# A decode kernel's first weight load, split by partitions over two DMA queues

## The chip, the cores and the metric

The kernel runs on one core of one Trainium2 chip. The metric is device time in microseconds (us), from one launch. The kernel before was run three times: 126.8, 126.88 and 127.03 us, median 126.88 us. A further execution was taken with the hardware profiler; its own time is 126.89 us, and all durations below are from it.

## The reference

One token `x` of 576 numbers is normalised (`xn`), sent through two branches, and their sum with `x` is the output. Everything is bfloat16.

```python
# attention branch: 32 query heads, 16 key/value heads, the last W = 4096 of 65536 cached rows
q = (xn @ wq)                        # wq: 576 x 4096
k, v = k_cache[:, :, Sk - W:, :], v_cache[:, :, Sk - W:, :]   # 16 heads x 4096 x 128 each
p = softmax(q . k * Dh ** -0.5);  o = p . v
attn = o @ wo                        # wo: 4096 x 576
# gated MLP branch
z = gelu(xn @ w_in)                  # w_in: 576 x 4608
z1, z2 = z[:2304], layernorm(z[2304:])
mlp = (z1 * (w_sp * z2 + b_sp)) @ w_out   # w_out: 2304 x 576
out = x + attn + mlp
```

There is one token, so every weight and every cached key and value is read once and used for one vector. The kernel reads 50.96 MB from memory.

## The kernel before

**What is loaded.** All the large loads are issued on one queue, SP's (`nc.sync.dma_start`, in the helpers `rows`, line 82, and `load_kv`, line 88). Each covers all 128 partitions with one contiguous row per partition. In order: the first 2 of each partition's 9 half rows of `wq` (8 KB per partition, 1 MB in all, tile `rest`), the other 7 half rows (28 KB per partition, tile `wq`), the key groups `k0` and `k1` (32 KB per partition, 4 MB each), `w_in` in two loads (tiles `win` and `rest`), `k2`, `v0`, `k3`, `v1`, `v2`, `v3`, `w_out` and, in five loads, `wo`. These 18 loads share four slots of SBUF (tags a, b, c, d), so that a later load waits on SP until the last reader of its slot is done; `k2`, for example, waits for the transposes of `k0`.

**What else is loaded.** On ACT's queue (`nc.scalar.dma_start`, lines 112 to 117) come `x`, in three pieces of 192 numbers, and the two scalars `w_sp` and `b_sp`. At the end the output leaves by the same queue (line 482).

**How the work goes.** The order on each engine is the order of the program (`tc.manual_schedule()`); nothing is moved by a scheduler. DVE clears constants and PSUM tiles (lines 123 to 170), copies `x` into `xtw` (line 181), nine small matmuls turn it into a column (line 183), and a chain of small operations (lines 187 to 209) makes the normalised `XT`. Then `wq` is multiplied, first the two half rows in `rest`, then the seven in `wq` (line 217), the query is spread (lines 222 to 245, ending in `Qb`), and per group of four heads `g` the keys are transposed on DVE in two halves (`keys`, line 258), scored (`scores`, line 265), put through the softmax (`sm_a`, `sm_b`), multiplied with the values (`pv`, line 329) and normalised (`tail`). `z_mms` (line 365) does `w_in` between groups; `out_mms` (line 465) does `w_out` and `wo` at the end and finishes as the last rows of `wo` land.

**Semaphores.** Each DMA raises one of eight semaphores, which are handed round; a DMA that gets one already used waits on its issuing engine until the earlier use has landed. In the kernel before, `k1` waits in this way for a piece of `x`.

Of the kernel before, what the change touches and what calls it, by code (L numbers as in the profile page):

```python
# [14 lines left out]
D = 576  # L15
# [11 lines left out]
NR = 98  # L27
NF = FH // 128
CUT = (0, 264, D)
XP = D // 3  # L30
EPS = 1e-5
SCALE = DH ** -0.5
GELU_C = 0.7978845608028654
# [4 lines left out]
def kernel(  # L38
# [14 lines left out]
    nc = tc.nc  # L53
    P = nc.NUM_PARTITIONS
# [16 lines left out]
    x_flat = A_x.flatten_outer_dims()  # L71


    def rows(slot, src, name, lo, n, at=None):

        w = src.shape[1]
        if at is None:
            t = big.tile([P, n * w], BF16, name=f"{name}{lo}", tag=slot)[:]
        else:
            t = slot[:, at:at + n * w]  # L80
        v = t.rearrange("p (s c) -> p s c", c=w)
        nc.sync.dma_start(v, src.rearrange("(p s) c -> p s c", p=P)[:, lo:lo + n, :])  # L82
        return [(lo + s, v[:, s, :]) for s in range(n)]

    def load_kv(slot, src, g, name):

        t = big.tile([P, TP * DH], BF16, name=f"{name}{g}", tag=slot)
        nc.sync.dma_start(t[:], src[0, GK * g:GK * g + GK, SK - W:SK, :].rearrange("h (r t) d -> r h (t d)", t=TP))
        return t[:].rearrange("p (t d) -> p t d", d=DH)

    wq_h = A_wq.rearrange("r (e c) -> (r e) c", e=2)
    win_h = B_w_in.rearrange("r (e c) -> (r e) c", e=2)
    K, V = {}, {}
    rest = big.tile([P, TP * DH], BF16, name="rest", tag="d")
    wq_sb = rows(rest, wq_h, "wq", 0, 2, 0) + rows("a", wq_h, "wq", 2, 7)
    K[0] = load_kv("b", A_k_cache, 0, "k")
    K[1] = load_kv("c", A_k_cache, 1, "k")
    win_sb = rows("a", win_h, "win", 0, 7) + rows(rest, win_h, "win", 7, 2, 4096)
    K[2] = load_kv("b", A_k_cache, 2, "k")
    V[0] = load_kv("c", A_v_cache, 0, "v")  # L100
# [3 lines left out]
    V[3] = load_kv("c", A_v_cache, 3, "v")  # L104
    ends = [big.tile([P, TP * DH], BF16, name=f"end{n}", tag="ad"[n]) for n in range(2)]
    wout_sb = rows(ends[0], B_w_out, "wout", 0, NF, 0)
    wo_sb = []
    for n, t, at in ((14, 1, 0), (9, 1, 14), (6, 0, NF), (2, 0, NF + 6), (1, 0, NF + 8)):
# [1 line left out]


    xrow = const.tile([1, D], BF16, name="xrow")
    for n in range(3):
        nc.scalar.dma_start(xrow[:, XP * n:XP * (n + 1)], x_flat[:, XP * n:XP * (n + 1)])
    spb = const.tile([1, 2], BF16, name="spb")
    nc.scalar.dma_start(spb[:, 0:1], B_w_sp.flatten_outer_dims()[0:1, 0:1])
# [396 lines left out]
```

## Time and profile before

| what | value |
|---|---|
| median of three runs | 126.88 us (126.8 to 127.03) |
| the profiled execution's own time | 126.89 us |
| its span, first to last instruction | 125.1 us |
| read from memory | 50.96 MB, 407 GB/s over the span |
| busy: PE, DVE, ACT, POOL | 70.8, 78.5, 43.2, 7.1 us |
| first load: issued, landed | 0.73 us, 4.8 us after issue |
| second load (`wq`): issued, landed | 1.15 us, 12.8 us after issue |
| `x` in use on DVE from | 7.32 us |
| `XT` ready, first `wq` matmul | 12.57 us |

Times inside the profile count from the span's start. The span is 1.8 us shorter than the execution's own time; what lies around it is launch and end. A DMA has three stages in the profile: the issuing engine works on the instruction (SPq or ACTq), the 16 DMA engines move packets (here one packet per partition row, and one of 4 bytes per DMA and engine that raises the semaphore), and the waiting engine goes on after the landing. The profile names the DMA queues by number: q1 is SP's, q10 is ACT's, q8 and q14 are instruction fetches. "DMA share" is the time that packets took as a share of 16 engines; a packet's bytes are counted where it starts, so in short windows the figures jump.

### The profile page before, as it was taken

How to read it: one execution, taken by the hardware profiler on the slowest of the kernel's cores; microseconds unless marked ns; L12 is line 12 of the kernel's file. 1: busy time of each engine (PE TensorE's matmuls, PEld its weight loads, DVE VectorE, ACT ScalarE, POOL GpSimd, SP SyncE). 2: the span in 40 equal slices, each digit the busy share in tenths (PEclk: the TensorE clock that was granted, in tenths of full speed). 3: DMA queues.
4: the chain of work that ended last, by engine and by line, in shares of the span. 5: the costliest groups of instructions: out<-in, count | busy, mean ns of one | idle time of the engine just before them, and what ended most of it. 6: DMA issues, size and time to landing. Idle time of an engine off the chain costs nothing.

```text
span 125.1 us, 1617 instructions
## 1 busy us (share of the span) xinstructions
PE 70.8 (57%) x626; PEld 28.9 (23%) x626; DVE 78.5 (63%) x150; ACT 43.2 (34%) x101; POOL 7.1 (6%) x19
## 2 busy tenths in 40 slices
PE   0012841009878469998390992059892932049992
PEld 0001201001101013998000131002211411015850
DVE  6745025899799976308999367999938359003301
ACT  2100011000000956996069008707801941940001
POOL 2961000000000000000000000000000100000000
PEclk9999998555995867755559599657998555555899
DMA  4999899998999999898999989999999999999960
GB/s 118 511 422 440 385 471 440 398 492 356 487 420 402 385 493 461 377 492 372 461 451 398 482 367 477 401 451 430 409 482 398 451 394 440 418 413 416 428 237 0
DMA packets 2611, 51.06 MB, mean 408 GB/s; under 512 B 299, under 2 KB 428, under 8 KB 684
## 3 DMA queue, kind: packets, MB, share of 16 engines
q1 hardware_dynamic: 2592, 50.96, 95.2%
q8 instruction: 5, 0.08, 0.2%
q14 instruction: 2, 0.02, 0.0%
q10 hardware_dynamic: 12, 0.00, 0.0%
HBM read 50.96 MB, written 0.00 MB: 407 GB/s over the span
## 4 chain that ended last, share of the span: by engine, by line
DMA 61%; DVE 30%; PE 5%; SPq 1%; issue 1%; ACT 0%; DVEq 0%
DMA k<-in_A_k_cache_dram 37%; DMA end<-in_A_wo_dram 25%; DVE kT L258 22%; DVE pt L303 4%; PE S L265 3%; PE acc L465 1%; SPq L82 1%; DVE mx L286 1%; DVE on L343 1%; DVE om L339 1%; PE yps L350 0%; ACT res L481 0%; DVE rs L320 0%; DVE mt L275 0%; DVE mb L281 0%
## 5 line engine op out<-in xcount | busy, mean ns | idle before, releaser
L265 PE MATMUL S<-kT,Qb 128*8 128x512 bf16 x128 | 32.5, 1148 | 23.3 <-DVE kT L258 22.8
L258 DVE STREAM_TRANSPOSE kT<-k 128x1024 f32<-128x1024 f32 x32 | 36.8, 1207 | 6.5 <-DMA k<-in_A_k_cache_dram 6.5
L292 ACT ACTIVATE pz<-S,nm 32x1024 bf16<-32x1024 f32 x16 | 19.1, 1192 | 33.6 <-DVE nm L289 20.6
L306 ACT COPY PT<-pt 32x128 f32<-32x128 f32 x64 | 19.8, 309 | 17.2 <-DVE pt L303 16.5
L329 PE MATMUL ops<-v,PT 128*32 128x512 bf16 x128 | 11.0, 505 | 6.8 <-ACT PT L306 6.8
L265 PEld LDWEIGHTS <-Qb 128*8 128x8 bf16 x128 | 3.5, 96 | 45.0 <-issue 34.8
L303 DVE STREAM_TRANSPOSE pt<-pz 128x1024 f32<-128x1024 f32 x8 | 9.4, 1210 | 0.8 <-ACT pz L292 0.8
L339 DVE SCALAR_TENSOR_TENSOR om<-ops,rs,dmask 128x512 f32<-128x512 f32 x4 | 3.0, 750 | 10.5 <-PE ops L329 10.3
L365 PEld LDWEIGHTS <-win 128*128 128x128 bf16 x126 | 7.9, 165 | 1.9 <-issue 1.9
L365 PE MATMUL zps<-XT,win 128*128 128x2 bf16 x126 | 8.0, 202 | 0.0
L286 DVE TENSOR_REDUCE mx<-S 128x1 f32<-128x1024 f32 x4 | 4.9, 1214 | 3.9 <-PE S L265 3.9
L329 PEld LDWEIGHTS <-PT 128*32 128x32 bf16 x128 | 3.7, 117 | 11.5 <-ACT PT L306 6.9
L226 ACT CAST q_rep<-qps 128x512 bf16<-128x512 f32 x2 | 1.2, 586 | 14.9 <-DVE q_rep L228 14.9
L404 POOL TENSOR_TENSOR mz<-mz,mhalf 128x1 f32<-128x1 f32 x1 | 0.6, 554 | 85.5 <-DVE mz L403 85.5
L183 PE MATMUL ps_x<-ones_b,xtw 1*128 1x1 bf16 x9 | 0.4, 162 | 8.7 <-DVE xtw L181 8.7
L465 PE MATMUL acc<-end,Y 128*1 128x312 bf16 (+1 forms) x64 | 4.9, 285 | 0.3 <-DMA end<-in_A_wo_dram 0.3
L228 DVE CAST q_rep<-qps 128x512 bf16<-128x512 f32 x2 | 1.4, 692 | 5.1 <-PE qps L217 4.5
L481 ACT CAST res<-acc 1x312 bf16<-1x312 f32 x1 | 0.4, 411 | 11.7 <-PE acc L465 11.7
L350 PE MATMUL yps<-on,sel 128*32 128x32 f32 x32 | 2.0, 210 | 4.1 <-DVE on L343 4.1
L343 DVE TENSOR_REDUCE on<-om 128x128 f32<-128x512 f32 x4 | 4.2, 1042 | 0.1
L480 DVE CAST res<-acc 1x264 bf16<-1x264 f32 x1 | 0.4, 420 | 5.2 <-PE acc L465 5.2
L465 PE MATMUL acc<-end,hv 128*1 128x264 bf16 (+1 forms) x36 | 3.6, 360 | 0.0
(92 smaller groups left out, 56.6 us busy)
## 6 DMA issues: line engine op xcount, KB each, us to landing
k<-in_A_k_cache_dram SPq DMA_DIRECT2D x4, 4096.0 KB
v<-in_A_v_cache_dram SPq DMA_DIRECT2D x4, 4096.0 KB, 26.0
win<-in_B_w_in_dram SPq DMA_DIRECT2D x1, 4032.0 KB, 27.1
wq<-in_A_wq_dram SPq DMA_DIRECT2D x1, 3584.0 KB, 12.8
end<-in_B_w_out_dram SPq DMA_DIRECT2D x1, 2592.0 KB, 22.3
end<-in_A_wo_dram SPq DMA_DIRECT2D x1, 2016.0 KB
end<-in_A_wo_dram SPq DMA_DIRECT2D x1, 1296.0 KB
rest<-in_B_w_in_dram SPq DMA_DIRECT2D x1, 1152.0 KB
```

Of the source, the lines that this page charges most:

```text
L258: nc.vector.transpose(dst[:, 1024 * n:1024 * (n + 1)], src[:, 1024 * n:1024 * (n + 1)])
L265: nc.tensor.matmul(S[g % 2][32 * x:32 * x + 8, c, :], lhsT=Qb[:, GK * g + x, be].rearrange("p a h -> p (a h)"), rhs=kv[:, be // 2, be % 2, x],
L286: nc.vector.tensor_reduce(out=mx[:, 0:1], in_=s[:], op=ALU.max, axis=mybir.AxisListType.XY)
L292: nc.scalar.activation(pz[lo:hi, :, :, x, :], s[lo:hi].rearrange("p a (t r e) -> p (a t) r e", r=8, e=2), ACT.Exp, bias=nm[lo:hi, 0:1], sc ...
L303: nc.vector.transpose(dst[:, 1024 * n:1024 * (n + 1)], src[:, 1024 * n:1024 * (n + 1)])
L306: nc.scalar.copy(PT4[32 * a:32 * a + 32, :, x, :], pt[32 * x:32 * x + 32, :, 2 * a:2 * a + 2])
L329: nc.tensor.matmul(ops[32 * q:32 * q + 32, :], lhsT=d["PT"][:, t0 // 2:t0 // 2 + 2].rearrange("p t x h e -> p (t x h e)"), rhs=V[g][:, t0: ...
L339: nc.vector.scalar_tensor_tensor(out=om[:].rearrange("p c d -> p (c d)"), in0=ops[:], scalar=d["rs"][:, 0:1], in1=dmask[:].rearrange("p c ...
L343: nc.vector.reduce_sum(on[:], om[:].rearrange("p c d -> p d c"), axis=AXX)
L350: nc.tensor.matmul(yps[32 * g:32 * g + 32, :], lhsT=sel[:, dq, :], rhs=d["on"][:, 32 * dq:32 * dq + 32], start=(dq == 0), stop=(dq == 3), ...
L365: nc.tensor.matmul(zps[:, :, t], lhsT=wt[:, t, :], rhs=XT[:, s, :], start=(s == 0 and t == 0), stop=(s == NS - 1 and t == NF - 1), skip_gr ...
L465: nc.tensor.matmul(acc[n], lhsT=lhs[:, col:col + 1], rhs=wv[:, CUT[n]:CUT[n + 1]], start=False, stop=last, tile_position=(0, 32 * n))
```

## The change

The first load is issued as two: partitions 80 to 127 (48 rows) on ACT's queue and partitions 0 to 79 (80 rows) on SP's. ACT's part stands ahead of `x` on ACT's queue. `x` comes in two pieces of 288 numbers where it came in three of 192, so the number of DMAs is the same as before. Nothing is computed differently. The lines behind the helper move by two.

```diff
-XP = D // 3
+XP = D // 2
...
-    def rows(slot, src, name, lo, n, at=None):
+    def rows(slot, src, name, lo, n, at=None, queues=((nc.sync, 0, P),)):
...
-        nc.sync.dma_start(v, src.rearrange("(p s) c -> p s c", p=P)[:, lo:lo + n, :])
+        sv = src.rearrange("(p s) c -> p s c", p=P)
+        for q, p0, p1 in queues:
+            q.dma_start(v[p0:p1], sv[p0:p1, lo:lo + n, :])
...
-    wq_sb = rows(rest, wq_h, "wq", 0, 2, 0) + rows("a", wq_h, "wq", 2, 7)
+    wq_sb = rows(rest, wq_h, "wq", 0, 2, 0, ((nc.scalar, 80, P), (nc.sync, 0, 80))) + rows("a", wq_h, "wq", 2, 7)
...
-    for n in range(3):
+    for n in range(2):
         nc.scalar.dma_start(xrow[:, XP * n:XP * (n + 1)], x_flat[:, XP * n:XP * (n + 1)])
```

In the order of the changed program, every other instruction of every engine stands where it stood. On SP, the issue of `k1` waits for one of the two first loads, whose semaphore it takes over, where it waited for a piece of `x`; `v1` waits in addition for the landing of one of the two scalars.

## The prediction

> **What bounds the kernel now.** I read the page's slices first, then its queues, then the chain that ended last in order of time, then the start in the timeline.
>
> From the page, the span in 40 slices, and its list of queues (packets, MB, share of 16 engines):
>
> ```profile
> DMA  4999899998999999898999989999999999999960
> GB/s 118 511 422 440 385 471 440 398 492 356 487 420 402 385 493 461 377 492 372 461 451 398 482 367 477 401 451 430 409 482 398 451 394 440 418 413 416 428 237 0
> ...
> q1 hardware_dynamic: 2592, 50.96, 95.2%
> ```
>
> The DMA engines are busy from the second slice to the last but one; only the first slice (3.1 us) is half empty. Nearly everything they do is SP's queue, q1.
>
> From the chain in order of time (start, length, what), its seven longest pieces:
>
> ```profile
> 1.62 22.00 DMA k<-in_A_k_cache_dram
> 23.65 9.14 DVE kT L258 x8
> 32.81 23.86 DMA k<-in_A_k_cache_dram
> 56.69 4.62 DVE kT L258 x4
> 64.32 4.55 DVE kT L258 x4
> 78.18 4.53 DVE kT L258 x4
> 90.41 30.86 DMA end<-in_A_wo_dram
> ```
>
> The long DMA pieces do not wait for an issue; they wait in line. `k2`, issued at 32.81, lands at 56.67, 23.86 us later, though its 4.19 MB take 10 us at the 407 GB/s of the page. The rest of the time is what was queued ahead of it. So the end is the start of the stream, plus 50.96 MB at its pace, plus the tail behind the last landing (121.27 to 125.1). A delay of the stream at its start moves everything by its own size: the landing of `k2`, for which DVE has waited 5.4 us (the longest of DVE's three waits for keys), so the DVE chain behind it, and the last rows of `wo`. Compute ahead of `k2` has slack instead, 5.4 us there.
>
> The change touches the first 5 us. The timeline has:
>
> ```profile
> 0.73 1.04 ACTq L114 DMA_DIRECT2D xrow<-in_A_x_dram  x3
> 0.73 0.37 SPq L82 DMA_DIRECT2D rest<-in_A_wq_dram  x1
> 1.15 0.42 SPq L82 DMA_DIRECT2D wq<-in_A_wq_dram  x1
> ...
> 7.32 1.34 DVE L181 COPY xtw<-xrow 1x1152 bf16<-1x1152 bf16 x1 [1.31 <-DMA xrow<-in_A_x_dram]
> ...
> 12.57 1.02 PE L217 MATMUL qps<-rest,XT 128*2 128x512 bf16 x8 [0.83 <-DVE XT L208]
> ```
>
> and the start cut into half microseconds (the last two columns are the DMA share and GB/s):
>
> ```profile
> 1.70:2.20 0.50, 0.00 (x0) 0.00 (x0) 0.44 (x2) 0.00 (x0) 0.00 (x0) 1.00 1.33 246
> 2.20:2.70 0.50, 0.00 (x0) 0.00 (x0) 0.50 (x4) 0.24 (x1) 0.00 (x0) 1.00 0.61 180
> 2.70:3.20 0.50, 0.00 (x0) 0.00 (x0) 0.50 (x5) 0.50 (x1) 0.16 (x1) 1.00 0.89 360
> 3.20:3.70 0.50, 0.00 (x0) 0.00 (x0) 0.29 (x2) 0.50 (x1) 0.50 (x2) 1.00 0.97 410
> 3.70:4.20 0.50, 0.00 (x0) 0.00 (x0) 0.50 (x1) 0.04 (x1) 0.44 (x4) 1.00 1.00 426
> ```
>
> The first large packet starts at 1.73, a full microsecond after SP took up the instruction, and the stream is at its pace only from about 3. Up to 4.5 the queue list counts 0.94 MB; from 3 to 4.5 the pace was 426 GB/s, at which 0.94 MB take 2.21 us, and 2.77 us passed. **The ramp loses 0.56 us.** In the packet records the engines' first packets start spread over 1.73 to 2.15, and many of them take 0.5 to 1.05 us where an 8 KB packet takes 0.31 later. So part of the loss is the handing-out of rows to 16 engines (the spread), part is waiting for the first bytes (the length).
>
> **The change, part by part.** The sum is made against the profiled execution, 126.89 us; the median is 126.88, so nothing is to be converted.
>
> *Issue.* SP's instruction for 128 rows takes 0.37 us, those of 192 numbers on ACT 0.21 to 0.50. For 80 rows I take 0.31 (0.16 us more than the smallest for 127 more rows, scaled to 80), so 0.06 us earlier. Ends: 0 and 0.16. I take **0.06**.
>
> *Hand-out.* Two queues hand out 5 and 3 rows per engine side by side, so that each engine has work after the shorter of them. If the spread of 0.42 us goes with the number of rows, it becomes 0.42 x 48/128 = 0.16, and the mean engine starts (0.42 - 0.16)/2 = 0.13 us sooner. Ends: 0 (one shared unit hands out, or the first bytes are the limit) and 0.56 (the whole ramp goes). I take **0.13**, since the spread is the only row that is surely hand-out.
>
> *Two queues at one engine.* This is new: in the first load each DMA engine has 5 rows on q1 and 3 on q10, and will take them in turn. No row of before has two bulk queues at once, so I bound it. From below: the small packets of `x` and of the scalars on q10 (384 bytes and less) slip in between `wq` packets on q1 at no cost; a 28 KB packet of q1 ahead of or behind one takes 1.06 us like all others. So 0. From above: instruction fetches, which come on q8 and q14 between q1's packets. The 16 KB packet at 36.47 took 0.94 us (0.61 at q1's pace), and the q1 packet behind it 1.69 where its fellows took 1.19; the engine fell back by 1.41 us, 0.80 more than the bytes. The 8 KB packet on q14 at 37.31 took its 0.31, but the q1 packet behind it 1.73 for 1.19: 0.53 lost for one excursion to another queue and back. Three rows on q10 are three excursions, so the upper end is 3 x 0.80 = 2.4 us. The nearest row by size is the 8 KB one: 3 x 0.53 = 1.59. One of the three falls into the ramp, where the engines wait for first bytes anyway, which leaves **1.06 us**. All 16 engines pay it, so the stream is late by it, and no backlog makes up for it.
>
> *`x`.* ACT now issues its 48 rows first, so `x` is issued from about 1.1 instead of 0.73. In the records the first piece of before got in ahead of the bulk (1.63); the second was served only at 4.72, when engine 0 had done its first load, and the third with one `wq` packet of 1.06 us between its steps, which is why DVE waits until 7.32. Two pieces behind the first load are four packets (data and semaphore each), as many as the second and third piece of before had, at the same place in the line: again about 7.3. This hides behind nothing it needs: the `wq` multiplication has 0.38 us until `wq` lands (13.95), and if `x` comes later than that the delay runs into DVE's waits for keys, 6.5 us in all. I take 0. The two scalars follow in the same order.
>
> *Waits on SP.* `k1` waits for a first load (the one of before landed 4.8 us after its issue, at 5.5) where it waited for a piece of `x`. Behind it on SP stands `win`, which waits until 17.18 anyway, and `k1` is needed in the line only when `k0` has gone through, at 23.6. `v1` waits for a scalar that landed by 11.6, and is issued after 59. Cost 0; if SP stood until 23, the stream would run dry.
>
> *Nothing else moves*: PE gets a second landing to wait for at the first `wq` matmul, long past by 12.57.
>
> **Sum: 126.89 - 0.06 - 0.13 + 1.06 = 127.76, forecast 127.8 us.** Its own range is 127.3 (half an excursion more than the ramp hides) to 128.3 (all three paid).
>
> **The rivals.**
>
> *The ramp shrinks and the turns are free* (faster). For it: q10's small packets cost q1 nothing, and the loss at the start is real. Against it: the first packets are slow in themselves, and a second queue does not bring the first bytes sooner. If excursions cost nothing and the whole ramp scales with the rows of the shorter part, 0.56 x 48/128 = 0.21 stays and 0.35 is won, with the issue 0.41: **126.5 us** (126.2 to 126.6). It decides if every engine's share of the first load is done by about 4.5 us.
>
> *Only the issue is won* (no change). Both parts go through the same 16 engines, so the start is as before but for 0.06: **126.83 us**. [...] The `x` packets agree as far as they show that q10 runs on an engine of q1; no run here shows more.
>
> *The parts collide at their targets* (slower still). In before every load spans all partitions and the 16 engines keep 0.31 us per 8 KB row without disturbing each other. A load of fewer partitions might not. If a half of the partitions takes rows only at half the pace (213 GB/s), the 48 rows, all in the upper half, take 1.85 us, the 64 of the 80 that lie in the lower half 2.46, one behind the other 4.31 where 128 rows take 2.46 now. That is 1.85 more: 126.89 - 0.19 + 1.85 = **128.55 us**. If the two interleave well it shrinks to nothing, so it decides by how the engines pair them; nothing in the trace speaks for or against it. [...]
>
> *`x` gets stuck.* If each of its four packets waits for several `wq` packets, `x` comes up to 8 x 1.06 = 8.5 us later; DVE's waits for keys swallow 6.5 us, and 2.0 come through with the above: 129.8 us. The third piece of before passed the queue with one packet between, which speaks against it.
>
> **How the numbers follow.** Chances: turns between queues (127.8) 0.38; collision 0.14; `x` stuck 0.02; ramp shrinks 0.33; only the issue 0.13. About 0.2% (0.25 us) is what a measurement of this kernel can tell from no change, so faster is below 126.63 and slower above 127.13. Faster 0.33, same 0.13, slower 0.54. The range reaches down to take in most of the faster case and up to the collision: 126.3 to 128.6 us.
>
> **What the profile of the changed kernel would show.** The windows from 1.7 to 4.5 and the packets up to 4.5: 0.94 MB or more by then means that the ramp shrank, less that turns or collisions cost. The first load's rows on q1 and q10: lengths of 0.31 with gaps or longer packets at each change of queue bear out the forecast; lengths of 0.6 all through, the collision. The landing of `wq` (13.95 now) and of `k2` (56.67) must move by the same amount as the end; if they do not, the sum is wrong in its frame. The `xtw` copy should start near 7.3. The forecast is wrong if `wq` lands at or before 13.95, and the whole argument if the end moves without it.

## The result, and the profile after

The changed kernel takes 128.36 us (median of 5 runs, 128.16 to 128.42); the kernel before, run beside it, 127.01 us (126.8 to 127.14). The ratio is 1.0105, with a 95% interval of 1.009 to 1.012: slower by 1.35 us. The profiled execution took 128.22 us, its span is 126.4 us (before 126.89 and 125.1). Two executions among the runs below, of 139.46 and 147.88 us, were in a slower state; medians and ratios are of the others.

The start in the timeline of the changed kernel:

```profile
0.73 0.42 ACTq L84 DMA_DIRECT2D rest<-in_A_wq_dram  x1
...
0.73 0.38 SPq L84 DMA_DIRECT2D rest<-in_A_wq_dram  x1
...
1.19 0.79 ACTq L116 DMA_DIRECT2D xrow<-in_A_x_dram  x2
...
9.08 1.34 DVE L183 COPY xtw<-xrow 1x1152 bf16<-1x1152 bf16 x1 [3.08 <-DMA xrow<-in_A_x_dram]
```

SP needs 0.38 us for 80 rows where it needed 0.37 for 128: nothing is won at the issue. `x` is taken up at 9.08, 1.76 us later than before. The same start in half microseconds (DMA share and GB/s last):

```profile
1.70:2.20 0.50, 0.00 (x0) 0.00 (x0) 0.44 (x2) 0.00 (x0) 0.00 (x0) 1.00 1.66 246
2.20:2.70 0.50, 0.00 (x0) 0.00 (x0) 0.50 (x4) 0.00 (x0) 0.00 (x0) 1.00 0.39 98
2.70:3.20 0.50, 0.00 (x0) 0.00 (x0) 0.50 (x5) 0.30 (x1) 0.16 (x1) 1.00 0.89 328
3.20:3.70 0.50, 0.00 (x0) 0.00 (x0) 0.29 (x2) 0.50 (x1) 0.50 (x2) 1.00 1.07 360
3.70:4.20 0.50, 0.00 (x0) 0.00 (x0) 0.50 (x1) 0.49 (x1) 0.44 (x4) 1.00 1.13 262
4.20:4.70 0.50, 0.00 (x0) 0.00 (x0) 0.34 (x2) 0.00 (x0) 0.50 (x4) 1.00 0.89 246
4.70:5.20 0.50, 0.00 (x0) 0.00 (x0) 0.50 (x1) 0.00 (x0) 0.50 (x2) 1.00 1.08 262
5.20:5.70 0.50, 0.00 (x0) 0.00 (x0) 0.45 (x2) 0.00 (x0) 0.50 (x1) 1.00 1.00 246
```

Two things are to be seen. Up to 3.2 the start is no faster than it was: the three windows add up to 336 KB, before to 393. From 3.7 to 5.7 the stream stands at 246 to 262 GB/s, where before ran at 410 to 467 from 3.2 to 4.7, and the DMA share is still 0.89 to 1.13: the engines are not idle between packets; each packet is slow. In the packet records the 8 KB packets of that stretch last 0.46 to 0.62 us, for 0.31 before, all 16 engines at once. The last first-load packet ends at 6.36 (before 5.17), and the first packet of the second load on each engine still takes 1.41 us in the mean, for 1.06. The second load starts on the mean engine at 6.04 instead of 4.90 (1.14 later), plus 0.35 for its slow first packet: 1.49. The landing of `wq` agrees, 15.48 (issue 1.18 plus 14.3) for 13.95.

The DMA pieces among the seven longest of the chain, and DVE's waits for keys:

```profile
1.64 23.51 DMA k<-in_A_k_cache_dram
...
34.33 23.80 DMA k<-in_A_k_cache_dram
...
92.60 29.95 DMA end<-in_A_wo_dram
```

```profile
DVE kT L260 <- DMA k<-in_A_k_cache_dram: 6.8, 3, 5.4
```

`k0` lands 1.53 us later than before, `k2` 1.46, and the last packet of the stream ends 1.35 us later by the packet records. So what is lost in the first 7 us goes through to the end, as the frame of the prediction had it; and DVE still waits for keys as long as before (6.8 us, before 6.5), so that the late `x` is hidden there.

### The profile page after: what moved, and what is told of

Read it like the earlier page. It is cut to its first block, busy times and chain, and to the rows that moved or that the text cites. A ratio compares the mean times of both kernels' runs of the same rounds, so it can differ in the third digit from the quotient of the medians.

```text
span 126.4 us, 1619 instructions
## 1 busy us (share of the span) xinstructions
PE 70.4 (56%) x626; PEld 29.4 (23%) x626; DVE 78.6 (62%) x150; ACT 43.2 (34%) x101; POOL 7.0 (6%) x19
## 4 chain that ended last, share of the span: by engine, by line
DMA 61%; DVE 22%; PE 12%; SPq 2%; issue 1%; ACT 0%
DMA k<-in_A_k_cache_dram 37%; DMA end<-in_A_wo_dram 24%; DVE kT L260 18%; PE S L267 7%; PE ops L331 3%; DVE pt L305 2%; SPq L84 2%; PE acc L467 1%; PE lps L314 1%; DVE on L345 1%; DVE om L341 1%; PE yps L352 0%; ACT res L483 0%; PE acc L441 0%; DVE u L376 0%
## 5 line engine op out<-in xcount | busy, mean ns | idle before, releaser
L267 PE MATMUL S<-kT,Qb 128*8 128x512 bf16 x128 | 32.9, 1159 | 23.1 <-DVE kT L260 23.0
L331 PE MATMUL ops<-v,PT 128*32 128x512 bf16 x128 | 10.4, 479 | 6.8 <-ACT PT L308 6.8
L467 PE MATMUL acc<-end,Y 128*1 128x264 bf16 (+1 forms) x64 | 4.9, 286 | 0.9 <-DMA end<-in_A_wo_dram 0.9
L467 PEld LDWEIGHTS <-Y 128*1 128x1 bf16 x64 | 3.4, 83 | 2.3 <-issue 1.8
## 6 DMA issues: line engine op xcount, KB each, us to landing
wq<-in_A_wq_dram SPq DMA_DIRECT2D x1, 3584.0 KB, 14.3
```

The source lines that it names most:

```text
L267: nc.tensor.matmul(S[g % 2][32 * x:32 * x + 8, c, :], lhsT=Qb[:, GK * g + x, be].rearrange("p a h -> p (a h)"), rhs=kv[:, be // 2, be % 2, x],
L331: nc.tensor.matmul(ops[32 * q:32 * q + 32, :], lhsT=d["PT"][:, t0 // 2:t0 // 2 + 2].rearrange("p t x h e -> p (t x h e)"), rhs=V[g][:, t0: ...
L467: nc.tensor.matmul(acc[n], lhsT=lhs[:, col:col + 1], rhs=wv[:, CUT[n]:CUT[n + 1]], start=False, stop=last, tile_position=(0, 32 * n))
```

## The experiments

The question is why the packets are slow. The forecast said: because each engine takes turns between two bulk queues. The rival: because a load over a part of the partitions collides at its targets. Some of the expectations weigh two forms of the collision, both of them assumptions that no row of before shows. By span: each half of the partitions takes rows at half the pace. By pairing: engines that work on a partial load meet at the same small group of partitions, wherever it lies. The times of before in this section are those beside which each kernel ran, 126.84, 126.95 and 126.81 us.

**Both parts on one queue.**

```diff
-    wq_sb = rows(rest, wq_h, "wq", 0, 2, 0, ((nc.scalar, 80, P), (nc.sync, 0, 80))) + ...
+    wq_sb = rows(rest, wq_h, "wq", 0, 2, 0, ((nc.sync, 0, 80), (nc.sync, 80, P))) + ...
```

> The changed kernel with both parts of the first load (80 rows, then 48) on SP's queue; x stays in two pieces on ACT's queue. No second bulk queue is left, the two partial loads are. Turns between queues: the loss goes, about 127.0 us, and the packets of the first load last 0.31 us once the start is over. Collision of partial loads at their targets: the loss stays, packets of 0.45 us and more, 128.2 to 128.9 us.

Measured: 129.29 us, ratio 1.0182 (1.0162 to 1.0203). The second queue is gone and the loss has grown, to 2.3 us by the ratio. Its stretches, GB/s last:

```profile
3.20:4.20 1.00, 0.00 (x0) 0.00 (x0) 0.79 (x2) 0.20 (x1) 0.94 (x5) 1.00 1.18 304
4.20:5.20 1.00, 0.00 (x0) 0.00 (x0) 0.84 (x2) 0.00 (x0) 1.00 (x5) 1.00 1.23 262
5.20:6.20 1.00, 0.00 (x0) 0.00 (x0) 0.94 (x3) 0.00 (x0) 1.00 (x1) 1.00 1.39 250
```

It is slow in the same way, and for longer. Two queues are not needed for the loss; on two queues, with the parts in turn, it was smaller. SP is also done with issuing `k1` at 3.35 here, where it stood on it until 7.2 in the changed kernel, so that wait is not the cause either.

**Two queues, both over all partitions.**

```diff
-    wq_sb = rows(rest, wq_h, "wq", 0, 2, 0, ((nc.scalar, 80, P), (nc.sync, 0, 80))) + ...
+    wq_sb = (rows(rest, wq_h, "wq", 0, 1, 0, ((nc.scalar, 0, P),)) + rows(rest, wq_h, "wq", 1, 1, 2048)
+             + ...
```

> The first load is cut by half rows and not by partitions: half row 0 of all 128 partitions on ACT's queue, half row 1 of all 128 partitions on SP's, 4 KB per packet. Two bulk queues stay, the partial loads go. Turns between queues: eight changes of queue per engine where the changed kernel has three, so at least its loss, 128.3 us or more. Collision: no loss, 126.7 to 127.2 us; if two queues also shorten the start, somewhat under before's 127.0.

Measured: 126.94 us, ratio 1.0011 (1.0002 to 1.002).

```profile
2.20:2.70 0.50, 0.00 (x0) 0.00 (x0) 0.50 (x4) 0.00 (x0) 0.00 (x0) 1.00 0.66 164
2.70:3.20 0.50, 0.00 (x0) 0.00 (x0) 0.50 (x5) 0.24 (x1) 0.16 (x1) 1.00 0.90 360
...
3.70:4.20 0.50, 0.00 (x0) 0.00 (x0) 0.50 (x1) 0.50 (x1) 0.44 (x4) 1.00 1.04 426
```

With two bulk queues and full width the stream runs at 426 GB/s and the loss is 0.1 us. The turns do take place: in the packet records each engine goes from one queue to the other row by row, and a 4 KB row takes 0.16 us, half of what 8 KB take. That takes the turns out of the sum. It also shows what a second queue does for the ramp, with no collision in the way: nothing is won, as the pace from 2.2 to 3.2 us is that of before or less (164 and 360 GB/s for 180 and 360).

**The whole first load on ACT's queue.**

```diff
-... ((nc.scalar, 80, P), (nc.sync, 0, 80))) + ...      # x in two pieces
+... ((nc.scalar, 0, P),)) + ...                         # x in three pieces
```

> The whole first load, all 128 partitions in one DMA, moves to ACT's queue ahead of x (three pieces); SP starts with the second load. Turns between queues: the engines have both queues filled, with 8 KB packets on one and 28 KB on the other, eight changes, so a loss of at least 1.3 us, 128.3 us or more. Collision: all loads have all partitions, so no loss from that, 126.8 to 127.3 us; x comes later by some us, which the waits of DVE for keys hide.

Measured: 135.48 us, ratio 1.0679 (1.0652 to 1.0706). Neither expected time holds, and the profile says why:

```profile
4.00:8.00 4.00, 0.00 (x0) 0.00 (x0) 1.79 (x3) 0.40 (x1) 4.00 (x7) 1.00 0.96 414
8.00:12.00 4.00, 0.00 (x0) 0.00 (x0) 0.00 (x0) 0.00 (x0) 0.34 (x3) 1.00 0.96 415
```

```profile
21.64 1.34 DVE L183 COPY xtw<-xrow 1x1152 bf16<-1x1152 bf16 x1 [15.64 <-DMA xrow<-in_A_x_dram]
```

The stream is at full pace while the 8 KB packets of one queue and the 28 KB packets of the other go in turn (0.31 and 1.06 us in the median, as alone). The first rows of `k0` start at 13.6 us on the mean engine, before at 13.4, so the turns cost 0.2 us at most here. But `x` stands behind eight such turns, is used only at 21.64, and this time the slack is not enough: DVE no longer waits for keys at all (6.5 us before), and the page's slices show the stream down at 156 to 161 GB/s around 67 to 74 us, where SP waits for slots to come free (`k3` is issued at 71.23, at 59.06 in the kernel before). I had put `x` at "some us" and the loss at nothing; `x` was 14.3 us late, and 8.6 us were lost.

**The second load split as well.**

```diff
+    wq_sb += rows("a", wq_h, "wq", 2, 7, None, ((nc.scalar, 80, P), (nc.sync, 0, 80)))   # behind x and the scalars
```

> The changed kernel with the second load (28 KB per partition) split 80 to 48 over the two queues as well, its ACT part behind x and the scalars. Collision: the loss goes with the bytes that are in partial loads, 36 KB per partition for 8, so 4.5 times 1.35, about 133 us, packets of 28 KB at 1.5 us and more where they take 1.06 now. Turns between queues: it goes with the number of changes, three more per engine, so about twice 1.35, 129.7 us.

Measured: 141.18 us, ratio 1.1122 (1.11 to 1.1145). It is on the collision's side, but the loss is 14.3 us, not 6.

```profile
2.72 30.18 DMA wq<-in_A_wq_dram
```

Two things add up in it. The stream is late: the first rows of `k0` start at 24.5 us on the mean engine, 11.1 later than before. In the packet records SP's 28 KB packets take 1.91 to 2.13 us until ACT's rows come in, the doubling that a half pace gives; ACT's then take 2.4 to 3.0 on 15 engines at once, and from 8 to 12 us the stream makes 136 GB/s where before makes 423. Why ACT's rows fall below a half I did not settle. The other thing is not pace: the last two of ACT's rows run on one engine at 25.79 and 29.14 us, in turn with rows of `k0`, so that `wq` lands at 32.9 (before 13.95). DVE's waits for keys, 6.5 us before, are down to 0.4: the slack is used up, as it was with `x` above. So the 14.3 us are no measure of the collision alone.

**Halves on two queues; halves on one queue.**

```diff
-... ((nc.scalar, 80, P), (nc.sync, 0, 80)) ...
+... ((nc.scalar, 64, P), (nc.sync, 0, 64)) ...      # two queues
+... ((nc.sync, 0, 64), (nc.sync, 64, P)) ...        # one queue
```

> The changed kernel with the first load split at partition 64: 64 rows on SP's queue, 64 on ACT's. Collision by span (each half of the partitions takes rows at half the pace): no half is covered by both parts, so if the engines work on both parts at once little is lost, under 0.7 us, and if they work on one after the other 2.4 us are lost as with two parts on one queue. Collision by pairing (engines that get rows of a partial load meet at the same group of partitions, whichever rows these are): each queue's rows pair the engines two and two, and taking the queues in turn lets one of a pair work on either half, so about half of the changed kernel's loss, 127.5 us.

> Both halves, partitions 0 to 63 and then 64 to 127, on SP's queue, x in two pieces on ACT's. Collision by span and by pairing alike: one half after the other, each at half the pace, 2.0 to 2.5 us lost, 128.9 to 129.4 us. Turns between queues, if anything is left of them: no loss, 127.0 us.

Measured: 128.97 us on two queues, ratio 1.0151 (1.0109 to 1.0192), and 129.22 us on one, 1.0175 (1.0159 to 1.019). The stretch from 4.2 to 5.2 us on two queues:

```profile
4.20:5.20 1.00, 0.00 (x0) 0.00 (x0) 0.84 (x2) 0.09 (x1) 1.00 (x5) 1.00 0.91 213
```

That is half the pace, and the 8 KB packets from 3.2 us on take 0.60 us in the median (0.61 on one queue), about twice 0.31. On two queues the engines did not take turns in the profiled execution: in the packet records ACT's rows run from 2.07 to 5.01 and SP's from 4.13 to 7.39. That is the branch "one after the other" of the span, and the pairing is wrong, which had expected 127.5. Why 80 and 48 rows were taken in turn and 64 and 64 not stays open. The four executions on two queues lie in two pairs, 128.36 and 128.53, 129.40 and 129.43 us; the profile is from the upper pair, so what the engines did in the lower one is not known.

**Even and odd partitions.**

```diff
+            if p1 > P:
+                q.dma_start(v[p0:P:2], sv[p0:P:2, lo:lo + n, :])
...
+... ((nc.scalar, 1, P + 1), (nc.sync, 0, P + 1)) ...
```

> The changed kernel with the first load split by even and odd partitions, 64 rows on SP's queue and 64 on ACT's. Collision by span: each part reaches from partition 0 to 127, so nothing is lost, 126.8 to 127.2 us. Collision by pairing: even and odd rows of one group lie side by side, the engines pair on both queues at the same groups, and nothing is won by taking turns, 128.9 to 129.3 us, packets of 0.5 us and more.

Measured: 127.4 us, ratio 1.0037 (1.0024 to 1.0051).

```profile
0.73 0.55 SPq L85 DMA_DIRECT2D rest<-in_A_wq_dram  x1
```

```profile
3.20:4.20 1.00, 0.00 (x0) 0.00 (x0) 0.79 (x2) 0.85 (x1) 0.94 (x5) 1.00 0.99 401
4.20:5.20 1.00, 0.00 (x0) 0.00 (x0) 0.84 (x2) 0.43 (x1) 1.00 (x5) 1.00 1.05 446
```

64 rows again, one queue after the other again, but reaching over all partitions, and the pace is full: the 8 KB packets take 0.31 us. What matters is which partitions a load covers, not how many rows it has. The 0.45 us that are left were lost at the start: the issue takes 0.55 us, the first packet starts at 2.07 instead of 1.73, 0.34 later, and the second load starts on the mean engine at 5.36 instead of 4.90. That part of the loss also lies in the two kernels with halves, whose first packets start at 2.07 and 2.08.

**Targets or sources.** Even and odd partitions also come from other rows in memory than two halves. So the split at 64 once more, with the sources of the even and odd split:

```diff
+            if p1 - p0 == 64:
+                q.dma_start(v[p0:p1], sv[p0 // 64:P:2, lo:lo + n, :])
```

> The kernel split at partition 64 on two queues, with other sources: partitions 0 to 63 get the even rows of the source, 64 to 127 the odd ones (the rows of wq are therefore multiplied with the wrong numbers; the work is the same). The targets are those of the split in halves, the sources those of the split in even and odd partitions. Collision at the targets: as the split in halves, 128.4 to 129.4 us, packets of 0.5 us and more. Collision at the sources in memory: as even and odd, 127.2 to 127.7 us, packets of 0.31 us.

Measured: 129.18 us, ratio 1.0184 (1.0169 to 1.0199).

```profile
3.20:4.20 1.00, 0.00 (x0) 0.00 (x0) 0.79 (x2) 0.91 (x1) 0.94 (x5) 1.00 1.04 246
4.20:5.20 1.00, 0.00 (x0) 0.00 (x0) 0.84 (x2) 0.38 (x1) 1.00 (x5) 1.00 1.03 238
```

With the sources of the fast split and the targets of the slow one it is slow, though the engines take the queues in the same order as in the fast one, SP's rows first: the targets decide.

**Half the bytes.**

```diff
+    wq_sb = (rows(rest, wq_h, "wq", 0, 1, 0, ((nc.scalar, 80, P), (nc.sync, 0, 80)))
+             + rows(rest, wq_h, "wq", 1, 1, 2048) + ...
```

> The changed kernel with only the first half row (4 KB per partition) split 80 to 48 over the two queues; the second half row follows on SP's queue as a load of its own over all partitions. Collision: half the bytes are in partial loads, so about half of the changed kernel's 1.35 us is lost, 127.5 to 127.8 us. Turns between queues, if anything is left of them: as many changes of queue as before, 1.35 us.

Measured: 127.33 us, ratio 1.0045 (1.0029 to 1.0061), 0.57 us lost, a little under half of 1.35, with as many changes of queue per engine. The loss went down with the bytes in partial loads.

**`x` ahead, and `x` in one piece.**

```diff
+    xrow = const.tile([1, D], BF16, name="xrow")
+    for n in range(2):
+        nc.scalar.dma_start(xrow[:, XP * n:XP * (n + 1)], x_flat[:, XP * n:XP * (n + 1)])
     wq_sb = rows(rest, wq_h, "wq", 0, 2, 0, ((nc.scalar, 80, P), (nc.sync, 0, 80))) + ...
```

> The changed kernel with x issued ahead of ACT's 48 rows instead of behind them. x lands some us sooner (DVE takes it up at 9.08 in the changed kernel; here before 7), and if its lateness costs nothing, as all theories say, the time stays at 128.4 us. If the lateness is part of the loss, the time falls by up to 1.35 us.

Measured: 130.17 us, ratio 1.0254 (1.0214 to 1.0294). The expectation was wrong because the edit does more than it says: ACT's 48 rows are now issued at 1.55 instead of 0.73, come into the line behind the first two packets of SP's second load on each engine (7.22 to 12.34 in the packet records) and collide with the next ones, which take 1.36 to 1.77 us for 1.06. Even so `x`, in use at 6.04, did not bring the time down; but the edit does not isolate it. A clean edit for that:

```diff
-XP = D // 2      # for n in range(2)
+XP = D           # for n in range(1)
```

> The changed kernel with x in one piece behind ACT's 48 rows, so two packets where there were four. x should land about 2.1 us sooner, as it no longer has two packets of the second load (1.06 us each) between its own. If its lateness is hidden by the waits for keys, the time stays within 0.2 us of 128.4; if it is part of the loss, the time falls below 128.1.

Measured: 128.28 us, ratio 1.0117 (1.0096 to 1.0138), with `x` in use 2.33 us sooner:

```profile
6.75 1.34 DVE L183 COPY xtw<-xrow 1x1152 bf16<-1x1152 bf16 x1 [0.75 <-DMA xrow<-in_A_x_dram]
```

The time does not follow `x`.

## Why the prediction was right in its sign and wrong in its mechanism

The measured 128.36 us lie within the stated range and on the forecast's side, 1.35 us slower for a forecast of 0.87. But the 127.8 stood on a mechanism that the runs refute, and the rival with 0.14, the collision, is what happened. That sign and size came out is luck: a cost of 1.06 us that does not exist stood in the sum in place of one that does.

- *The frame* held: a delay of the stream at its start moves `wq` (1.53 us), `k0` (1.53), `k2` (1.46) and the end (1.35) by nearly its own size.
- *Issue, 0.06 us*: nothing. 80 rows took 0.38 us, 128 rows 0.37.
- *Hand-out, 0.13 us*: nothing. The first packet starts at 1.75 (before 1.73), those of the 16 engines come by 2.31, and ACT's rows only from 2.43. That the spread is the handing-out of rows was my reading, and no run isolates it. The spread of before was also read too short: 2.15 is the 15th engine's first packet, and the 16th's, if the packets are followed engine by engine, starts at 2.63. The kernel with two queues over all partitions has no shorter ramp (164 and 360 GB/s from 2.2 to 3.2 us, before 180 and 360). The rival "the ramp shrinks" falls with it.
- *Two queues at one engine, 1.06 us*: this is the step that failed; the runs show about 0 for it. I priced a change of queue by the instruction fetches, the nearest row by size; the page lists those as another kind (`instruction`, the loads as `hardware_dynamic`). The rows at the other end, the small packets of `x`, were right: in the kernel before they took 0.01 to 0.02 us, and the 28 KB packets beside them 1.06 as alone. Two full-width bulk queues lose 0.1 us, and 8 KB against 28 KB packets in turn keep their 0.31 and 1.06 us. The lower end of the forecast's own range, 127.3, does not follow either: one excursion paid gives 126.70 + 0.53 = 127.2.
- *In its place, the collision*: from 4.2 to 5.2 us the kernels with the whole first load in partial loads ran at 213 to 262 GB/s (but for the one with `x` ahead, where 28 KB packets of the second load come in between), the rival's half pace (213) and a little better. No row of before showed that half pace; it was an assumption of the rival. Its price of 1.85 us is for 80 and 48 rows one behind the other; on one queue they come so, and 2.3 us were lost. Halves by the same sum cost 2.46, and 2.0 and 2.3 were lost. With 80 and 48 rows in turn on two queues 1.35 were lost; that the two parts then overlap in part is my reading, and no run isolates it. That the loss is at the targets is shown by the pair of even and odd partitions (127.4) and interleaved sources (129.18). On two queues 1.35 us were lost with 80 and 48 rows, 2.0 with halves and 0.45 with even and odd rows; why rows for a block of partitions come at about half the pace is in no trace here. The halves on two queues ran one after the other in the profiled execution (2.07 to 5.01, then 4.13 to 7.39); the 80 and 48 rows did not, as the engines took them in turn.
- *`x`, 0 us*: the cost was right, the time was not. I had 7.3, it was 9.08. Its four packets stood where I had put them, with two packets of the second load between; but the line ahead was longer by the collision.
- *Waits on SP*: `k1` was issued late (SP stood on it until 7.2), and nothing was late for it; with both parts on SP it was issued by 3.35, and the loss was larger.

## What to carry to other kernels

When a load is split, split it so that each part still covers partitions of the whole range (by columns, 126.94 us here, or by even and odd rows, 127.4): here parts that cover a block of partitions moved at 213 to 262 GB/s from 4.2 to 5.2 us, on one queue or two, and parts that reach over the whole range at 401 to 446 from 3.2 to 5.2 (even and odd rows) and at 401 to 426 from 3.2 to 4.7 (by columns). A second queue did not shorten the start of the stream here; the first packets are slow with one queue (0.49 to 1.05 us for the first 15 packets of the kernel before, 0.31 later) and with two (0.56 to 1.10 for the first 16 of the changed kernel). And what stood behind a bulk part on a queue waited a turn for each of its packets: `x` behind eight rows per engine was in use at 21.64 us, 7.32 in the kernel before. So a small load that a long chain needs belongs ahead of the bulk part, unless that pushes the bulk part into the next one, as it did with `x` ahead (130.17 us for 128.36).

## What the runs showed that I had not expected

- A DMA of 64 rows took longer to issue than one of 80 or 128: 0.55 to 0.59 us (0.60 each for two in a row) against 0.38 and 0.37, and its first packet started at 2.07 to 2.09 us instead of 1.73 to 1.75. This holds for halves and for even and odd rows.
- The partial loads slowed the full load behind them: in the changed kernel the first 28 KB packet of each engine took 1.28 to 1.52 us for 1.06.
- Engines with two bulk queues took 80 and 48 rows in turn, 64 and 64 one queue after the other (in the three profiled executions with 64 rows on each queue).
- A load that landed late cost little until DVE's waits for keys (6.5 us) were used up (`x` in use at 9.08 and at 6.75: 128.36 and 128.28 us), and much after that, as with `x` at 21.64 (135.48 us) and `wq` at 32.9 (141.18 us).
- No version tried beats the kernel before.
